# Linear attention whose state is kept compact, 64x64 a head, with a fused update out of PSUM

## The chip, the cores and the metric

The kernel runs on one core of one Trainium2 chip. What is measured is the device time of one execution, in microseconds. Engines are named as the profile names them: PE is TensorE's matmul, PEld its weight load, DVE is VectorE, ACT is ScalarE, POOL is GpSimd, SP is SyncE, which issues most of the DMAs.

## What is computed

Three layers stand one behind the other: a linear attention with a decaying state, a mixture of eight experts of which each token takes one, and a gated feed-forward layer. Only the first is touched:

```python
B, H, S, D = r.shape                      # 4, 8, 768, 48
state = np.zeros((B, H, D, D))
for t in range(S):
    kt, vt, rt = (k[:, :, t], v[:, :, t], r[:, :, t])
    cur = np.einsum('bhd,bhe->bhde', u[None] * kt, vt)
    y[:, :, t] = np.einsum('bhd,bhde->bhe', rt, state + cur)
    state = w[None, :, :, None] * state + np.einsum('bhd,bhe->bhde', kt, vt)
```

The 4 x 768 tokens of 384 = 8 x 48 numbers then go through the experts (384 to 1024 to 384) and through the last layer (384 to 1536 to 384), all in float32.

## The kernel before

**Tiles.** The attention works on tiles of 128 tokens: six tiles make one batch element, and four of those make 24 tiles. In a tile the eight heads lie as four pairs (`NP = 4`). A pair takes 128 partitions: head j of a pair has its 48 dimensions in partitions 64j to 64j + 47, and the 16 behind them are padding. Within a tile the recurrence over time is replaced by products. With `pw[t]` the decay to the power t, r is multiplied by the powers (`rdT`, on DVE) and k by their inverses (`kdT`, and token by token `kdc`, on POOL).

**The steps of one tile, by function.** `scores` forms k by r for each head (`pss`, L406): the two heads of a pair use 64 rows of the array each and write two PSUM banks. DVE then copies the masked scores into `dsb`, which already holds the diagonal term with u (L410). `state` forms the tile's sum of k by v in `pskv` (L428, one 48x48 product a head, the two heads of a pair side by side in the columns of the array) and brings the state forward: it adds `pskv` to the old state (L435) and multiplies the sum by the tile's whole decay `w128` (L441), once for each half j of the partitions. `outputs` multiplies the state by `rdT` (L453) and the values by `dsb` (L460) into one PSUM tile `psy`, which ACT copies to `yT` (L465). `rows_out` and `emit` (L114 to L127) form the gate's logits and store the rows.

**The state's form.** `st_b` is two buffers of 128x(4x128). Each pair has a 128x128 block that is zero but for two 48x48 squares on its diagonal, one a head, so that one 128x128 product serves both heads. POOL clears both buffers at the start (L332), and only the squares are ever written. The DVE instructions of `state` work on 48 partitions and 4x48 columns.

**What sets the order.** PE, DVE, ACT and POOL issue the attention in program order. One round of the loop over i runs: `scaled_r(i+1)`, `bonus(i+1)`, `scores(i)`, `state(i-1)`, `scaled_k(i+2)`, `outputs(i-1)`, `rows_out(i-2)`. What a product of the state in `outputs` reads was thus written a round earlier. Between these steps `advance()` issues, one at a time, small DVE instructions that sort the finished batch element's tokens to their experts (`route`, `gate`); `state` calls it after each of its DVE instructions, twice where `i >= HURRY` (18). The first tile of a batch element (c = 0) has no old state, and the last (c = 5) forms no new one. Both the experts and the last layer come behind the attention.

Of the kernel before, what the change touches and what calls it, by code (L numbers as in the profile page):

```python
# [9 lines left out]
F32 = mybir.dt.float32  # L10
# [5 lines left out]
ALU = mybir.AluOpType  # L16
# [4 lines left out]
P = 128  # L21
# [15 lines left out]
def moe_kernel(ctx, tc, cst, small, tok, tr, u, w1, w2, m_gate, m_val, m_out, out):  # L37
    nc = tc.nc
    NT, DM = out.shape
    H, D = u.shape  # L40
# [3 lines left out]
    NP = H // 2  # L44
# [19 lines left out]
    ident, mask, iota_p, niota, rev8, slot, tokid, tile_i, part_i, ltm = (  # L64
        cs[:, at[n]] for n in ("ident", "mask", "iota", "niota", "rev", "slot", "tokid", "tile", "part", "ltm")
    )
# [196 lines left out]
    with ExitStack() as actx:  # L263
# [53 lines left out]
        for q in range(NP):  # L317
            nc.vector.tensor_tensor_scan(
                out=pw[:, q, 1:], data0=wc[:, q : q + 1].to_broadcast([P, P]), data1=ones,
                initial=1.0, op0=ALU.mult, op1=ALU.mult,  # L320
            )
            nc.vector.reciprocal(wkT[:, q, :], pw[:, q, 1:])
        pst = ps_m.tile([P, NP, P], F32, name="pst", tag="m")
        for q in range(NP):
            nc.tensor.transpose(pst[:, q, :], wkT[:, q, :], ident)
        wk_tok = carve(H * D).rearrange("p (h d) -> p h d", d=D)
        nc.scalar.copy(wk_tok, pst.rearrange("p q (j d) -> p (q j) d", j=2)[:, :, 0:D])

        nc.gpsimd.memset(yd_all[:, used[0] :], 0.0)
        st_b = [acst.tile([P, NP, P], F32, name=f"st{i}") for i in range(2)]  # L330
        for t in st_b:
            nc.gpsimd.memset(t, 0.0)  # L332
        w128 = pw[:, :, P : P + 1].to_broadcast([P, NP, D])
        nc.vector.memset(rows_f, 0.0)
        nc.vector.memset(cum[:, 0:1, :], 0.0)

# [11 lines left out]
        def inputs(i):  # L348
            t = io[i % NIO]
            r_t, k_t = heads(t[:, 0 : RK // 2]), heads(t[:, RK // 2 : RK])  # L350
            rT, kT = pairs(t[:, RK : RK + T]), pairs(t[:, RK + T :])
            rdT = apool.tile([P, NP, P], F32, name="rdT", bufs=3)
            kdT = apool.tile([P, NP, P], F32, name="kdT", bufs=3)
            ck = apool.tile([P, H, D], F32, name="ck")
            kdc = apool.tile([P, H, D], F32, name="kdc", bufs=3)
            S[i] = r_t, k_t, rT, kT, rdT, kdT, ck, kdc

        def scaled_k(i):

            if i >= NTILE:  # L360
                return
            inputs(i)
            r_t, k_t, rT, kT, rdT, kdT, ck, kdc = S[i]
            if i == 0:
                for q in range(NP):
                    nc.gpsimd.tensor_tensor(out=kdT[:, q], in0=kT[:, q], in1=wkT[:, q], op=ALU.mult)
                    nc.gpsimd.tensor_tensor(out=rdT[:, q], in0=rT[:, q], in1=wrT[:, q], op=ALU.mult)
            eng = nc.vector if i < EARLY else nc.gpsimd
            eng.tensor_tensor(out=ck, in0=k_t, in1=u_tok, op=ALU.mult)
            eng.tensor_tensor(out=ck, in0=ck, in1=r_t, op=ALU.mult)  # L370
            if i:
                nc.gpsimd.tensor_tensor(out=kdT, in0=kT, in1=wkT, op=ALU.mult)
            nc.gpsimd.tensor_tensor(out=kdc, in0=k_t, in1=wk_tok, op=ALU.mult)

        def scaled_r(i):
            if i >= NTILE:
# [41 lines left out]
        def state(i):  # L418
            c = i % NCH
            if c + 1 == NCH:  # L420
                return
            rdT, kdT, kdc, dsb, v_t = S[i]
            st, st_n = st_b[i % 2], st_b[(i + 1) % 2]
            pskv = ps_m.tile([P, NP, 64], F32, name="pskv", tag="m")
            for q in range(NP):
                for j in range(2):
                    p0 = 64 * j
                    nc.tensor.matmul(  # L428
                        pskv[p0 : p0 + D, q, 0:D], lhsT=kdc[:, 2 * q + j, :], rhs=v_t[:, 2 * q + j, 0:D],
                        start=True, stop=True,  # L430
                    )
            js = [(slice(64 * j, 64 * j + D), slice(64 * j, 64 * j + D)) for j in range(2)]
            if c:
                for pr, cl in js:
                    nc.vector.tensor_tensor(out=st_n[pr, :, cl], in0=pskv[pr, :, 0:D], in1=st[pr, :, cl], op=ALU.add)  # L435
                    advance()
                    if i >= HURRY:
                        advance()
            for pr, cl in js:
                src = st_n[pr, :, cl] if c else pskv[pr, :, 0:D]  # L440
                nc.vector.tensor_tensor(out=st_n[pr, :, cl], in0=src, in1=w128[pr], op=ALU.mult)  # L441
                advance()
                if i >= HURRY:
                    advance()

        def outputs(i):
# [3 lines left out]
            psy = ps_y.tile([P, NP, P], F32, name="psy", tag="y")  # L450
            if c > 0:
                for q in range(NP):
                    nc.tensor.matmul(  # L453
                        psy[:, q, :], lhsT=st_b[i % 2][:, q, :], rhs=rdT[:, q, :], start=(q == 0), stop=False,
                        skip_group_check=True,
                    )
            for q in range(NP):
                for j in range(2):
                    p0 = 64 * j
# [912 lines left out]
```

## Time and profile before

| | |
|---|---|
| median of 3 runs | 865.82 us (865.14 to 867.04) |
| the profiled execution's own time | 865.42 us |
| its span, first to last instruction | 863.6 us |
| PE busy | 825.0 us, 96% of the span |
| DVE busy | 550.7 us, 64% |
| ACT busy | 348.7 us, 40% |
| POOL busy | 215.9 us, 25% |

The attention fills the first 160 us; the experts and the last layer fill the rest. A share of busy time is a mean over both. "Busy" counts an instruction from its start to its end, also where it is held up in between, and the records of PE overlap, since matmuls are pipelined. On PE one float32 product is two records.

### The profile page before, as it was taken

The numbers are of one execution on the slowest core, as the hardware profiler recorded it, in microseconds if no ns is written. First come the engines' busy times: TensorE is split into PE (matmuls) and PEld (weight loads), VectorE is DVE, ScalarE is ACT, GpSimd is POOL, SyncE is SP. The second block draws the span as 40 slices with busy tenths as digits, with TensorE's granted clock in tenths as the row PEclk, the third lists the DMA queues.
The fourth block names the chain that finished last, engine by engine and source line by source line (L and its number), as shares of the span: only waits on it lengthen the run. The fifth ranks groups of instructions, "written<-read, shape, count | busy, mean of one in ns | idle before, by whom it ended". The sixth has DMA issues, their size and how long they took to land.

```text
span 863.6 us, 14276 instructions
## 1 busy us (share of the span) xinstructions
PE 825.0 (96%) x5375; PEld 740.3 (86%) x5376; DVE 550.7 (64%) x1101; ACT 348.7 (40%) x789; POOL 215.9 (25%) x205
## 2 busy tenths in 40 slices
PE   7988877999999999999999999999999999999995
PEld 5766656899899999999888888888888888889995
DVE  8999999759999898974555333533533343344532
ACT  3665655446556646654343212211221221222321
POOL 7986764155334242110000200100010010001000
PEclk7998999999999999999999999999999999999998
DMA  8787766456688786642330100000010010001000
GB/s 302 258 304 230 261 229 206 132 170 195 194 277 241 250 256 212 199 123 68 110 95 27 38 1 1 31 18 1 13 37 2 1 33 10 1 8 38 1 20 22
DMA packets 61838, 99.55 MB, mean 115 GB/s; under 512 B 5364, under 2 KB 47872, under 8 KB 61760
## 3 DMA queue, kind: packets, MB, share of 16 engines
q1 hardware_dynamic: 58320, 88.44, 31.9%
q0 software_dynamic: 3440, 10.11, 3.6%
q8 instruction: 44, 0.72, 0.4%
q14 instruction: 34, 0.28, 0.1%
HBM read 82.00 MB, written 16.53 MB: 114 GB/s over the span
## 4 chain that ended last, share of the span: by engine, by line
issue 57%; DVE 18%; PE 13%; DMA 5%; POOL 3%; ACT 2%; SPq 0%; DVEq 0%; POOLq 0%; ACTq 0%
DMA m<-ab 3%; PE py L1068 3%; PE ph L1068 2%; POOL out_dram L1212 2%; DVE dsb L410 2%; DVE st L441 2%; DMA yd_all<-in_tr_dram 2%; DVE rdT L380 2%; DVE w1l L946 2%; DVE ab L922 1%; PE pya L1068 1%; PE psy L460 1%; PE psy L453 1%; DVE ab L918 1%; DVE h L1088 1%
## 5 line engine op out<-in xcount | busy, mean ns | idle before, releaser
L1236 DVE TENSOR_TENSOR hv<-pg,hv 128x512 f32<-128x512 f32 (+1 forms) x84 | 51.6, 615 | 156.8 <-ACT hv L1235 156.7
L1212 POOL DMA_INDIRECT out_dram<-ot,tokd x24 | 24.8, 1035 | 452.3 <-DVE ot L1211 448.7
L1235 ACT ACTIVATE hv<-pg 128x512 f32<-128x512 f32 (+1 forms) x84 | 45.1, 537 | 169.3 <-PE pg L1231 169.0
L854 ACT CAST hh<-hv 128x512 fp32r<-128x512 f32 (+1 forms) x84 | 47.0, 559 | 141.3 <-DVE hv L1237 141.3
L1205 PE MATMUL po<-wh,hh 128*128 128x384 f32 x288 | 97.1, 337 | 0.0
L1205 PE MATMUL po<-wh,hl 128*128 128x384 f32 x288 | 97.0, 337 | 0.0
L1205 PE MATMUL po<-wl,hh 128*128 128x384 f32 x288 | 97.0, 337 | 0.0
L1231 PE MATMUL pg<-xh,wh 128*128 128x512 f32 (+1 forms) x252 | 91.1, 362 | 0.0
L1068 PE MATMUL ph<-x,w1h 128*128 128x416 f32 x336 | 91.0, 350 | 0.0
L1231 PE MATMUL pg<-xh,wl 128*128 128x512 f32 (+1 forms) x252 | 90.9, 361 | 0.0
L1231 PE MATMUL pv<-xh,wh 128*128 128x512 f32 (+1 forms) x252 | 90.8, 360 | 0.0
L1231 PE MATMUL pv<-xh,wl 128*128 128x512 f32 (+1 forms) x252 | 90.7, 360 | 0.0
L1231 PE MATMUL pv<-xl,wh 128*128 128x512 f32 (+1 forms) x252 | 90.6, 360 | 0.0
L1231 PE MATMUL pg<-xl,wh 128*128 128x512 f32 (+1 forms) x252 | 90.5, 359 | 0.0
L1068 PE MATMUL py<-h,w2h 128*128 128x416 f32 x336 | 89.7, 352 | 0.0
L396 ACT ACTIVATE dsb<-cs,cb 128x128 f32<-128x128 f32 x192 | 58.8, 389 | 54.9 <-DVE cb L392 54.9
L855 DVE TENSOR_TENSOR hl<-hv,hh 128x512 fp32r<-128x512 f32 (+1 forms) x84 | 51.7, 616 | 45.4 <-ACT hh L854 45.1
L1237 DVE TENSOR_TENSOR hv<-pv,hv 128x512 f32<-128x512 f32 (+1 forms) x84 | 51.7, 615 | 43.4 <-PE pv L1231 42.7
L919 POOL TENSOR_TENSOR low<-low,exw 128x384 f32<-128x384 f32 x36 | 40.3, 1120 | 106.5 <-DVE exw L915 87.5
L1068 PEld LDWEIGHTS py<-h,w2h 128*128 128x128 f32 x336 | 62.9, 188 | 0.8
L1068 PEld LDWEIGHTS ph<-x,w1h 128*128 128x128 f32 x336 | 63.0, 188 | 0.5
L1068 PE MATMUL ph<-x,w1l 128*128 128x416 f32 x168 | 60.7, 361 | 2.6 <-DVE h L1088 2.6
(211 smaller groups left out, 1774.9 us busy)
## 6 DMA issues: line engine op xcount, KB each, us to landing
r<-in_w_dram SPq DMA_DIRECT2D x64, 384.0 KB
yd_all<-in_tr_dram SPq DMA_DIRECT2D x24, 512.0 KB
yd_all<-in_tok_dram SPq DMA_DIRECT2D x24, 384.0 KB
m<-ab SPq DMA_DIRECT2D x36, 192.0 KB
rw<-m SPq DMA_DIRECT2D x36, 192.0 KB
yd_all<-in_tok_dram SPq DMA_DIRECT2D x24, 256.0 KB
x_d<-xt SPq DMA_DIRECT2D x24, 192.0 KB
cva<-in_w_gate_dram SPq DMA_DIRECT2D x12, 384.0 KB
```

Of the source, the lines that this page charges most:

```text
L380: nc.vector.tensor_tensor(out=rdT, in0=rT, in1=wrT, op=ALU.mult)
L396: nc.scalar.mul(dsb[:, h, :], ident, cb[:, h : h + 1])
L854: first = nc.scalar.copy(hi, src)
L855: second = nc.vector.tensor_tensor(out=lo, in0=src, in1=hi.bitcast(F32), op=ALU.subtract)
L919: nc.gpsimd.tensor_tensor(out=low, in0=low, in1=ex.bitcast(F32), op=ALU.mult)
L1068: nc.tensor.matmul(dst[:, 0:n], lhsT=a, rhs=b, start=start and t == 0, stop=stop and t == 2)
L1205: nc.tensor.matmul(po[t], lhsT=a[:, t * P : (t + 1) * P], rhs=bb, start=(f == 0 and j == 0), stop=(f == KF2 - 1 and j == 2))
L1212: st = nc.gpsimd.indirect_dma_start(out=out[:, :], out_offset=bass.IndirectOffsetOnAxis(ap=tokd[:, i : i + 1].bitcast(U32), axis=0), in_=o ...
L1231: nc.tensor.matmul(dst, lhsT=a[:, fs], rhs=bb[:, q, :], start=(q == 0 and j == 0), stop=(q == KD - 1 and j == 2))
L1235: nc.scalar.activation(hv, pg, AF.Sigmoid)
L1236: nc.vector.tensor_tensor(out=hv, in0=pg, in1=hv, op=ALU.mult)
L1237: nc.vector.tensor_tensor(out=hv, in0=pv, in1=hv, op=ALU.mult)
```

## The change

The state is held as 128x(4x64): head j of pair q has its 64x64 square in partitions 64j to 64j + 63 and columns 64q to 64q + 63, and no zeros lie between. The decay of the whole tile is moved into the keys: `we` is the inverse powers times the power 128 (four ACT instructions in the set-up), and `wk_tok`, from which POOL makes `kdc`, is now the transpose of `we`. So `pskv` comes out already decayed, and one DVE `scalar_tensor_tensor` for a pair does old state times decay plus `pskv`: four instructions of 128x64 in place of four of 48x192. For c = 0 one copy of 128x256 takes the place of two multiplications. The products that form `pskv` are 64x64 instead of 48x48, for which `kdc` gets zero padding, written once into three standing buffers. The products that read the state are two of 64x64 for a pair, where one of 128x128 stood.

```diff
+        we = apool.tile([P, NP, P], F32, name="we", tag="yT")
+        for q in range(NP):
+            nc.scalar.mul(we[:, q, :], wkT[:, q, :], pw[:, q, P : P + 1])
         for q in range(NP):
-            nc.tensor.transpose(pst[:, q, :], wkT[:, q, :], ident)
+            nc.tensor.transpose(pst[:, q, :], we[:, q, :], ident)
...
-        st_b = [acst.tile([P, NP, P], F32, name=f"st{i}") for i in range(2)]
-        for t in st_b:
-            nc.gpsimd.memset(t, 0.0)
-        w128 = pw[:, :, P : P + 1].to_broadcast([P, NP, D])
+        st_b = [acst.tile([P, NP, 64], F32, name=f"st{i}") for i in range(2)]
+        kdc_b = [acst.tile([P, H, 64], F32, name=f"kdc{i}") for i in range(3)]
+        for t in kdc_b:
+            nc.gpsimd.memset(t[:, :, D:], 0.0)
...
-            nc.gpsimd.tensor_tensor(out=kdc, in0=k_t, in1=wk_tok, op=ALU.mult)
+            nc.gpsimd.tensor_tensor(out=kdc[:, :, 0:D], in0=k_t, in1=wk_tok, op=ALU.mult)
...
                     nc.tensor.matmul(
-                        pskv[p0 : p0 + D, q, 0:D], lhsT=kdc[:, 2 * q + j, :], rhs=v_t[:, 2 * q + j, 0:D],
+                        pskv[p0 : p0 + 64, q, :], lhsT=kdc[:, 2 * q + j, :], rhs=v_t[:, 2 * q + j, :],
                         start=True, stop=True,
                     )
-            js = [(slice(64 * j, 64 * j + D), slice(64 * j, 64 * j + D)) for j in range(2)]
-            if c:
-                for pr, cl in js:
-                    nc.vector.tensor_tensor(out=st_n[pr, :, cl], in0=pskv[pr, :, 0:D], in1=st[pr, :, cl], op=ALU.add)
-                    advance()
-                    if i >= HURRY:
-                        advance()
-            for pr, cl in js:
-                src = st_n[pr, :, cl] if c else pskv[pr, :, 0:D]
-                nc.vector.tensor_tensor(out=st_n[pr, :, cl], in0=src, in1=w128[pr], op=ALU.mult)
+            if c == 0:
+                nc.vector.tensor_copy(st_n, pskv)
+                advance()
+                advance()
+                return
+            for q in range(NP):
+                nc.vector.scalar_tensor_tensor(
+                    out=st_n[:, q, :], in0=st[:, q, :], scalar=pw[:, q, P : P + 1], in1=pskv[:, q, :],
+                    op0=ALU.mult, op1=ALU.add,
+                )
                 advance()
                 if i >= HURRY:
                     advance()
...
                 for q in range(NP):
-                    nc.tensor.matmul(
-                        psy[:, q, :], lhsT=st_b[i % 2][:, q, :], rhs=rdT[:, q, :], start=(q == 0), stop=False,
-                        skip_group_check=True,
-                    )
+                    for j in range(2):
+                        pr = slice(64 * j, 64 * j + 64)
+                        nc.tensor.matmul(
+                            psy[pr, q, :], lhsT=st_b[i % 2][pr, q, :], rhs=rdT[pr, q, :], start=(q == 0), stop=False,
+                            skip_group_check=True,
+                        )
```

Two places show what stands in a row. On DVE, in the fourth batch element, instructions of the sorting (`rk` to `sel`) lie between those of the state. Before:

```order
L127 TENSOR_REDUCE lg_1970<-psl_2019 128x16
L178 TENSOR_TENSOR rk<-psp,oh_all 128x48
L435 TENSOR_TENSOR st_160<-pskv,st_159 48x4x48
L181 TENSOR_REDUCE rank_all<-rk 128x6
L185 SCALAR_TENSOR_TENSOR num<-rank_all,at_e 128x6
L435 TENSOR_TENSOR st_160<-pskv,st_159 48x4x48
L189 TENSOR_SCALAR big<-num 128x6
L192 SCALAR_TENSOR_TENSOR npos<-big,num 128x6
L194 TENSOR_SCALAR col<-big 128x6
L441 TENSOR_TENSOR st_160<-st_160,yd_all 48x4x48
L199 TENSOR_TENSOR p_oh<-cs,npos 128x768
L202 TENSOR_TENSOR sel<-cs,col 128x192
```

The same place of the changed kernel:

```order
L127 TENSOR_REDUCE lg_2016<-psl_2065 128x16
L178 TENSOR_TENSOR rk<-psp,oh_all 128x48
L442 SCALAR_TENSOR_TENSOR st_165<-st_164,yd_all,pskv 128x64
L181 TENSOR_REDUCE rank_all<-rk 128x6
L185 SCALAR_TENSOR_TENSOR num<-rank_all,at_e 128x6
L442 SCALAR_TENSOR_TENSOR st_165<-st_164,yd_all,pskv 128x64
L189 TENSOR_SCALAR big<-num 128x6
L192 SCALAR_TENSOR_TENSOR npos<-big,num 128x6
L194 TENSOR_SCALAR col<-big 128x6
L442 SCALAR_TENSOR_TENSOR st_165<-st_164,yd_all,pskv 128x64
L199 TENSOR_TENSOR p_oh<-cs,npos 128x768
L202 TENSOR_TENSOR sel<-cs,col 128x192
```

The sorting's instructions keep their places; each of the four state instructions is exchanged for one of the new form.

On PE, one tile of the first batch element from its last product of the logits on. Before:

```order
L126 MATMUL psl_410<-cs,lT 128x128
L428 MATMUL pskv<-yd_all,kdc 48x48 x8
L453 MATMUL psy<-rdT,st_159 128x128 x4
L460 MATMUL psy<-dsb,yd_all 64x128 x8
L114 MATMUL psl<-yT,sm_t 32x128 x4
```

The same place of the changed kernel:

```order
L126 MATMUL psl_417<-cs,lT 128x128
L432 MATMUL pskv<-yd_all,kdc_168 64x64 x8
L459 MATMUL psy<-rdT,st_164 64x128 x8
L466 MATMUL psy<-dsb,yd_all 64x128 x8
L114 MATMUL psl<-yT,sm_t 32x128 x4
```

Nothing moves; four products of the state become eight, all into the tile `psy`.

## Rows read from the trace of the kernel before

**Rows 1.** Stretches, one per batch element: busy us (instructions) by engine, granted clock, DMA

```profile
23.20:53.80 30.60, 28.44 (x371) 22.50 (x370) 29.89 (x47) 21.16 (x68) 28.73 (x26) 0.96 0.74 254
53.80:89.90 36.10, 30.64 (x387) 24.43 (x386) 35.33 (x76) 19.44 (x59) 25.28 (x23) 0.91 0.78 260
89.90:130.50 40.60, 32.78 (x403) 26.22 (x403) 39.76 (x88) 24.14 (x72) 27.42 (x24) 0.92 0.71 244
130.50:160.00 29.50, 25.41 (x328) 20.73 (x329) 27.04 (x79) 16.48 (x52) 12.19 (x10) 0.94 0.53 177
```

The columns behind the stretch and its length are PE, PEld, DVE, ACT, POOL, then the granted clock as a share of full speed, the DMA engines' busy share and GB/s.

**Rows 2.** The same stretches, DVE instructions that touch the state alone: busy us (count)

```profile
23.20:53.80 30.60, 10.55 (x18) 0.96 0.74 254
53.80:89.90 36.10, 8.42 (x16) 0.91 0.78 260
89.90:130.50 40.60, 8.51 (x18) 0.92 0.71 244
130.50:160.00 29.50, 6.34 (x18) 0.94 0.53 177
```

**Rows 3.** The tile st: its DVE instructions, ns least/median/most

```profile
L435 DVE TENSOR_TENSOR st<-pskv,st x32: 324/351/361, 24.5 to 156.3; 48x192 f32<-48x192 f32 x32
L441 DVE TENSOR_TENSOR st<-st,yd_all x32: 340/382/1318, 25.2 to 157.1; 48x192 f32<-48x192 f32 x32
```

**Rows 4.** DVE's timeline in the first batch element: start us, length us, instruction

```profile
30.34 0.20 DVE L127 TENSOR_REDUCE lg<-psl 128x16 f32<-128x64 f32 x1
30.47 0.72 DVE L435 TENSOR_TENSOR st<-pskv,st 48x192 f32<-48x192 f32 x2
31.22 1.72 DVE L441 TENSOR_TENSOR st<-st,yd_all 48x192 f32<-48x192 f32 x2
32.97 1.38 DVE L380 TENSOR_TENSOR rdT<-yd_all 128x512 f32<-128x512 f32 x1
```

**Rows 5.** PE's timeline, one tile without a wait, at full clock

```profile
26.10 0.66 PE L120 MATMUL psx<-cs,yT 128*128 128x128 f32 x4
26.69 1.16 PE L406 MATMUL pss<-rdT,kdT 64*128 64x128 f32 x16
...
28.04 0.56 PE L428 MATMUL pskv<-yd_all,kdc 128*48 128x48 f32 x16
28.53 1.16 PE L453 MATMUL psy<-rdT,st 128*128 128x128 f32 x8
29.62 1.09 PE L460 MATMUL psy<-dsb,yd_all 128*64 128x128 f32 x16
...
31.00 0.66 PE L120 MATMUL psx<-cs,yT 128*128 128x128 f32 x4
```

**Rows 6.** PE's timeline behind a wait for the sorting, at the lower clock

```profile
74.44 0.48 PE L210 MATMUL psw<-sel,p_oh 128*128 128x64 bf16 x6 [2.89 <-DVE sel L206]
...
75.93 2.08 PE L453 MATMUL psy<-rdT,st 128*128 128x128 f32 x8
```

**Rows 7.** Groups by shape: DVE instructions with a PSUM input; busy us, mean ns

```profile
L1088 DVE SCALAR_TENSOR_TENSOR h<-ph,h 128x416 fp32r<-128x416 f32 x56 | 32.6, 581 | 5.1 <-ACT h L1087 4.9 <-issue 0.2
...
L1211 DVE COPY ot<-po 128x384 f32<-128x384 f32 x12 | 6.7, 557 | 12.9 <-DMA out_dram<-ot,tokd 10.7 <-PE po L1205 1.9
...
L1088 DVE SCALAR_TENSOR_TENSOR h<-pha,h 128x256 fp32r<-128x256 f32 x8 | 3.4, 423 | 3.1 <-ACT h L1087 2.6 <-issue 0.3
...
L212 DVE SCALAR_TENSOR_TENSOR rows_f<-psw,rows_f 128x32 f32<-128x32 f32 x4 | 0.7, 173 | 0.0
```

**Rows 8.** Timeline of the set-up: the token decay and the first kdc

```profile
8.78 0.48 ACT L327 COPY yd_all<-pst 128x384 f32<-128x384 f32 x1 [6.72 <-PE pst L325]
...
12.18 2.60 POOL L373 TENSOR_TENSOR kdc<-yd_all 128x384 f32<-128x384 f32 x2
```

**Rows 9.** Stretches behind the attention, columns as in the first group

```profile
160.00:200.00 40.00, 39.35 (x321) 37.35 (x318) 27.17 (x86) 21.66 (x56) 14.55 (x15) 1.00 0.55 166
200.00:350.00 150.00, 145.94 (x797) 138.99 (x797) 140.52 (x289) 88.54 (x174) 57.21 (x51) 1.00 0.76 236
```

More of the change, by code (lines that the diff above doesn't have):

```diff
@@ L354, in inputs @@
             ck = apool.tile([P, H, D], F32, name="ck")
-            kdc = apool.tile([P, H, D], F32, name="kdc", bufs=3)
+            kdc = kdc_b[i % 3]
             S[i] = r_t, k_t, rT, kT, rdT, kdT, ck, kdc
```

## The prediction

> **What bounds the kernel now.** I began with the stretches of the attention, one per batch element [rows 1]. In the first three DVE is busy 29.89 of 30.60 us, 35.33 of 36.10 and 39.76 of 40.60: 98% each time. PE is busy 28.44, 30.64 and 32.78 us of the same, POOL 28.73, 25.28 and 27.42. In the fourth DVE has 27.04 of 29.50 and PE 25.41. So the attention is set by DVE, with PE not far below. Behind it the rule is another: PE is busy 39.35 of 40 us and 145.94 of 150 [rows 9]. Those stages start when the attention hands over and run at PE's pace, so what the attention gains or loses should reach the end of the span almost whole.
>
> Then I took out DVE's part for the state [rows 2]: 10.55, 8.42, 8.51 and 6.34 us, together 33.8 of the 136.8 us. The reader is to see in [rows 3] that its two kinds of instruction behave differently at the same shape, 48x192. The addition, one input in PSUM and one in SBUF, takes 324 to 361 ns in all 32 cases. The multiplication, both inputs in SBUF, takes 340 to 1318 ns. In a plain tile of the first batch element two additions take 0.72 us and two multiplications 1.72 us [rows 4], while POOL is nearly always busy [rows 1]. `rdT`, which also reads two tensors of SBUF, follows there with 1.38 us. I read the excess as DVE being held while POOL works on SBUF.
>
> Last comes PE's floor, from a tile that it does without a wait at full clock [rows 5]: from one `psx` (26.10) to the next (31.00) is 4.90 us. The reader is to compare three products in it. The scores have 16 records of 64 rows and take 1.16 us. The values by `dsb`, 16 records of 64 columns, take 1.09. The state's product has only 8 records of the full array, and takes 1.16. So two products on different halves of the array's rows, or of its columns, run side by side and cost one.
>
> **The change part by part.** *DVE, the state.* Four instructions of 128x64 replace four of 48x192, in 16 tiles of 24. No row shows this form: one SBUF tensor, one PSUM tensor and a scalar for each partition. The nearest are `scalar_tensor_tensor` out of PSUM with a constant scalar [rows 7]: 173 ns at 32 columns, 423 at 256, 581 at 416. The last two give (581 - 423) / 160 = 0.99 ns a column, so 64 columns take 173 + 32 x 0.99 = 205 ns alone. In [rows 4] the addition starts at 30.47, 0.07 us before the `lg` in front of it ends at 30.54. Overlapped like this, one would follow the other after 0.13 us, and four cost 3 x 0.13 + 0.21 = 0.60 us. Back to back without overlap, as the two additions stand (0.72 us for two of 0.35), they cost 0.82. I take 0.60, since the two additions begin on different partitions and the new four on the same, as `lg` and the addition do. The ends for the range are 0.5 and 0.9. For c = 0 a copy out of PSUM takes 557 ns at 384 columns, so 557 - 128 x 0.99 = 0.43 us at 256, against about 0.7 for two of 0.35. A batch element then spends 4 x 0.60 + 0.43 = 2.8 us on the state instead of 10.55, 8.42, 8.51 and 6.34.
>
> *The state's products on PE.* Two 64x64 products for each pair use opposite halves of rows and columns at once, and both write the tile `psy`. No row shows that combination: pairs by rows write two banks (`pss`), and pairs by columns share all rows (`psy` from `dsb`). Both run side by side at the price of one, so I take 1.16 us as before. Below it there is little to find, since the columns that stream through are the same. The upper bounds are in the second rival. `pskv` streams 64 columns instead of 48: its 16 records in eight pairs take 0.56 us, at most a third more is 0.2, and I take 0.1. PE's floor for a tile is then 5.0 us, less 0.5 where c = 5 forms no `pskv`, and 5.0 - 1.1 = 3.9 where c = 0 has no state to read. Some 0.8 us for the sorting's products in all but the first batch element makes 4 x 5.0 + 4.5 + 3.9 = 28.4 or 29.2 us a batch element.
>
> The page "TensorEngine Tiling (Array Packing)" of the Trainium skill speaks against this part: its section on restrictions says that different row tiles can't use one PSUM bank at the same time. By that the two products of a pair would not run side by side, which is the second rival. The page "PSUM — Partial Sum Buffer" of the Trainium skill, in its section on bank collisions, calls the bank of each partition a RAM of its own and reports no clash between different groups of partitions in one bank, which is the case here; by that the price stays as I took it. No run here shows either yet.
>
> *POOL.* `kdc` has as many elements as before and only lands with gaps. I count zero, and 0.1 us more a tile as the upper end, which POOL's idle time in the later three stretches covers (10.8, 13.2 and 17.3 us [rows 1]). The three paddings replace two clearings before the first tile's inputs are there.
>
> *The set-up.* `wk_tok` now waits for four ACT scalings and is one step later. Before, its copy ends at 8.78 + 0.48 = 9.26, and `kdc` uses it first at 12.18 [rows 8]. The 2.9 us between cover the extra step, which at ACT's pace in the same row is about half a us. I count zero; without that cover it would cost 0.5 us.
>
> *The sum.* For each stretch I set DVE's busy time with the new state against PE's floor and take the later, plus what the two can't overlap. First stretch: DVE 29.89 - 10.55 + 2.8 = 22.1, PE 28.4, so PE decides: 30.6 becomes 28.4, a gain of 2.2. Second: DVE 35.33 - 8.42 + 2.8 = 29.7, PE 29.2. Two engines so even don't overlap wholly; I put 31, a gain of 5. Third: DVE 39.76 - 8.51 + 2.8 = 34.1, PE 29.2; I put 35, a gain of 5.6. Fourth: PE stands still for 29.50 - 25.41 = 4.1 us, and I take 2.5 of it. Together 15.3 us.
>
> From this I take back a part. A multiplication that no longer waits for POOL brings the next one with two SBUF inputs, mostly `rdT`, to POOL's instruction sooner, so some of the wait only moves. Read from [rows 2] and [rows 3], the state cost 8.42 us in the second stretch, where 16 instructions of 0.35 would be 5.6, and 8.51 in the third, where 18 would be 6.3: 5 us of waits in the two. I give back 3. So 12 us are gained: the profiled execution of 865.42 becomes 853.4, and since the median of the runs lies 0.4 above it, I predict **854 us**.
>
> The clock can add to the gain. In the second stretch PE waits 2.89 us for the sorting's `sel` and then runs the state's product in 2.08 us instead of 1.16, at the lower of the two clock levels (1.2 instead of 2.4 GHz) [rows 6, 5]. The granted clock of the four stretches is 0.96, 0.91, 0.92 and 0.94 [rows 1]. If shorter waits bring back half of what is missing, that is about 0.03 x 136.8 = 4 us. I leave it out of the sum and take it as the lower end.
>
> **The rivals.** *First: the freed time on DVE is taken by others.* DVE's waits for POOL then move whole, and POOL, with 28.73 busy of 30.60 us in the first stretch, holds its pace. For it speaks `rdT`, which is held in the tile shown. Against it, the additions were never held, and the new form has the same two kinds of input. The page "SBUF — State Buffer" of the Trainium skill, section on who interferes with whom, says that with at most one SBUF input there is no contention, but leaves open for me whether a scalar out of SBUF counts; by the rows it need not. Price: the gains of the second and third stretch shrink by the 5 us of waits, and with four instructions at 0.9 us by another 16 x 0.3 = 5. That leaves 15.3 - 10 = 5, and 2 if the first stretch gives nothing: 861 to 864 us.
>
> *Second: the two products of a pair take turns.* Place: PE, in `outputs`, 20 tiles. Taking turns, 16 records cost twice 1.16, so 1.1 us more a tile. PE's floor is then 28.4 + 5 x 1.1 = 33.9 in the first stretch, 3.3 above today's 30.6; the second comes to about 35 (a gain of 1), the third to 36.5 (4), and the fourth loses 2. All in all it comes to about zero: 866 us. From there on the kernel is **slower than before**. If each turn also costs what a change of the array's division does, the step grows further. The upper bound for that is the row at the lower clock: 2.08 for 8 records, thus 4.2 for 16, 3.0 more a tile. The stretches would be 28.4 + 15 = 43, 44, 44 and 25.4 + 15 = 40 us, 34 us slower, 900 us. The point at which it decides is 1.1 us a tile; I see 868 to 880 as its likelier part. Against it: pairs by rows and pairs by columns each run side by side [rows 5].
>
> *Third: the change gains more,* because the clock holds: 846 to 848 us, as worked out above.
>
> **How the numbers follow.** I give the forecast (849 to 860) 0.62, the third rival (below 849) 0.10, the first (860 to 864.1) 0.13, and taking turns 0.11: 0.05 for about the time before, 0.06 for slower. The rest, 0.04, is for causes that I don't see, half of them slower, half without an effect. A measurement of this kernel can tell a difference of about 0.2%, which is 1.7 us. Faster by more is 0.62 + 0.10 + 0.13 = 0.85, of which I move 0.03 to no change, since the first rival ends at the bound. So faster 0.82, same 0.05 + 0.02 + 0.03 = 0.10, slower 0.06 + 0.02 = 0.08. The range from 846 to 864 leaves out the second rival and a little below, less than 0.2.
>
> **What would show it.** In the changed profile the state's DVE instructions should sum to about 11 us, each near 0.2 us and none above 0.3; if many reach 1 us, the scalar counts as an SBUF input. The state's 16 records should take 1.1 to 1.2 us in a tile without a wait; 2.2 or more means that they take turns. A tile without a wait should take about 5.0 us on PE, the first scores of the experts should start some 12 us earlier, and the stages behind should last as long as before. The prediction is wrong if PE's waits for `sel` and for `dsb` stay as long as they are, or if the stages behind the attention give back what it gained.

## The result and the profile after

The changed kernel takes 855.67 us (median of 4 runs, 854.55 to 856.34), the kernel before 866.43 in the same series (865.14 to 867.65): a ratio of 0.9875, with an interval from 0.9856 to 0.9894. That is 10.8 us less, where 12 were forecast. The profiled execution took 855.75 us, with a span of 854.0, where before had 865.42 and 863.6. So the two traces differ by 9.6 us, and the stages below account for these. Over the whole span PE is busy for 820.0 us, DVE for 534.2, ACT for 350.9 and POOL for 215.7.

The same four stretches of the attention as in [rows 1], with the same columns, cut at the same work (the last one ends, as there, where PE starts on `psx` of the last tile but one):

```profile
22.60:50.40 27.80, 26.42 (x402) 20.73 (x398) 21.83 (x48) 23.59 (x74) 27.33 (x25) 1.00 0.88 298
50.40:82.30 31.90, 28.84 (x427) 22.99 (x426) 31.76 (x77) 18.91 (x57) 27.99 (x25) 0.95 0.84 290
82.30:120.20 37.90, 32.88 (x443) 26.22 (x443) 37.76 (x86) 24.19 (x72) 27.65 (x24) 0.91 0.77 261
120.20:148.48 28.28, 25.52 (x369) 20.27 (x369) 24.66 (x78) 16.48 (x52) 11.25 (x10) 0.94 0.56 185
```

They are 2.8, 4.2, 2.7 and 1.2 us shorter, 10.9 in all, and the first begins 0.6 us earlier. In the first, DVE now has room (21.83 of 27.80), while PE (26.42, at a granted clock of 1.00 where it was 0.96) and POOL (27.33) are both nearly full. Some of PE's records are missing there (402). A second profile of the same kernel, from the last run below, has 420 of them in the same stretch, and in it PE never stands still. POOL's busy time contains waits of its own: `kdc` takes 986 to 1712 ns at one shape.

```profile
22.36:50.10 27.74, 27.74 (x420) 22.00 (x416) 21.82 (x47) 23.51 (x74) 27.27 (x25) 0.98 0.89 297
```

In the second and third DVE is as full as before: 31.76 of 31.90 and 37.76 of 37.90. The state alone on DVE, as in [rows 2]:

```profile
22.60:50.40 27.80, 3.80 (x17) 1.00 0.88 298
50.40:82.30 31.90, 3.91 (x16) 0.95 0.84 290
82.30:120.20 37.90, 4.30 (x17) 0.91 0.77 261
120.20:148.48 28.28, 4.48 (x17) 0.94 0.56 185
```

That is 16.5 us where 33.8 stood. The tile `st`, as in [rows 3] (ns least, median, most):

```profile
L459 PE MATMUL psy<-rdT,st x320: 269/269/473, 21.6 to 146.9; 64*64 64x128 f32 x160
L442 DVE SCALAR_TENSOR_TENSOR st<-st,yd_all,pskv x64: 241/269/286, 24.4 to 144.2; 128x64 f32<-128x64 f32 x64
L437 DVE COPY st<-pskv x4: 403/406/446, 21.2 to 121.6; 128x256 f32<-128x256 f32 x4
```

All 64 fused updates lie between 241 and 286 ns, where the multiplications reached 1318: none is held, although beside 46 of them an instruction of POOL runs. DVE's timeline in a plain tile, to be read beside [rows 4]:

```profile
33.60 0.21 DVE L127 TENSOR_REDUCE lg<-psl 128x16 f32<-128x64 f32 x1
33.73 0.84 DVE L442 SCALAR_TENSOR_TENSOR st<-st,yd_all,pskv 128x64 f32<-128x64 f32 x4
34.49 1.76 DVE L384 TENSOR_TENSOR rdT<-yd_all 128x512 f32<-128x512 f32 x1
```

Four updates take 0.84 us where additions and multiplications took 2.5. With the last at 0.27, the other three follow at steps of (0.84 - 0.27) / 3 = 0.19. `rdT` behind them now takes 1.76 us instead of 1.38. PE's timeline, one tile without a wait, as in [rows 5]:

```profile
30.50 0.66 PE L120 MATMUL psx<-cs,yT 128*128 128x128 f32 x4
31.09 1.16 PE L410 MATMUL pss<-rdT,kdT 64*128 64x128 f32 x16
...
32.44 0.69 PE L432 MATMUL pskv<-yd_all,kdc 128*64 128x64 f32 x16
33.05 1.09 PE L459 MATMUL psy<-rdT,st 64*64 64x128 f32 x16
34.07 1.09 PE L466 MATMUL psy<-dsb,yd_all 128*64 128x128 f32 x16
...
35.45 0.66 PE L120 MATMUL psx<-cs,yT 128*128 128x128 f32 x4
```

From `psx` to `psx` it is 4.95 us. The state's 16 records of 64x64 take 1.09, so the two products of a pair run side by side, on opposite quarters of the array and in one bank. `pskv` takes 0.69 instead of 0.56.

The experts' first product, of the kernel before and then of the changed one (ns least, median, most, first and last start):

```profile
L1068 PE MATMUL pha<-x,w1l x24: 277/280/387, 161.6 to 176.0; 128*128 128x256 f32 x24
```

```profile
L1074 PE MATMUL pha<-x,w1l x24: 277/280/384, 150.1 to 164.5; 128*128 128x256 f32 x24
```

It starts 11.5 us earlier. A product of the last layer, in the same order, has its first 12.2 and its last 12.1 us earlier:

```profile
L1231 PE MATMUL pg<-xh,wl x252: 277/389/397, 402.9 to 849.2; 128*128 128x512 f32 x90, 128*128 128x256 f32 x36
```

```profile
L1237 PE MATMUL pg<-xh,wl x252: 277/389/397, 390.7 to 837.1; 128*128 128x512 f32 x90, 128*128 128x256 f32 x36
```

The span is only 9.6 us shorter, so 2.5 us are lost behind PE's last product. They lie in POOL's sequence at the very end, where a branch passes over the code for tokens that found no place. POOL's part of that line, before and then after:

```profile
L846 POOLq EVENT_SEMAPHORE  x4: 17/17/43, 856.2 to 856.4; - x4
...
L846 POOLq COMPARE_BRANCH  x1: 45/45/45, 855.7 to 855.7; - x1
```

```profile
L852 POOLq EVENT_SEMAPHORE  x4: 17/17/43, 846.6 to 846.8; - x4
...
L852 POOLq COMPARE_BRANCH  x1: 53/53/53, 843.6 to 843.6; - x1
```

From the branch to POOL's next instruction of that line it is 0.5 us before and 3.0 after. What follows, up to the end of the span, is as long in both (863.6 - 856.2 = 7.4 and 854.0 - 846.6 = 7.4).

### The profile page after: what moved, and what is told of

Same layout as the page of the kernel before. It is cut to its first block, busy times and chain, and to the rows that moved or that the text cites. A ratio compares the mean times of both kernels' runs of the same rounds, so it can differ in the third digit from the quotient of the medians.

```text
span 854.0 us, 14581 instructions
## 1 busy us (share of the span) xinstructions
PE 820.0 (96%) x5535; PEld 736.6 (86%) x5536; DVE 534.2 (63%) x1097; ACT 350.9 (41%) x793; POOL 215.7 (25%) x206
## 4 chain that ended last, share of the span: by engine, by line
issue 58%; DVE 16%; POOL 10%; PE 8%; DMA 5%; ACT 1%; SPq 0%; POOLq 0%; DVEq 0%; ACTq 0%
DMA m<-ab 3%; POOL out_dram L1218 2%; POOL kdT L376 2%; DVE w1l L952 2%; POOL kdc L377 2%; DMA yd_all<-in_tr_dram 1%; DVE ab L928 1%; DVE ab L924 1%; DVE dsb L414 1%; POOL ck L373 1%; DVE w2l L952 1%; DVE ab L919 1%; DVE rdT L384 1%; PE pya L1074 1%; DVE h L1094 1%
```

## The experiments

The theory after the result: the gain comes from DVE's update alone, the form of the products neither costs nor gives anything, and the rest of the freed DVE time is taken up because POOL and PE now limit together with DVE. The rival: the products, too, have a part in it, or DVE alone still sets the time. The medians below stand beside the kernel before in the same series, which took 868.94 us in the first group of runs (products alone, update alone, two steps, half the turns), 867.19 in the second (no update, update twice, decay on ACT, sorting later) and 865.52 in the last (the other four). The kernel before alone moves by 3.4 us from series to series, so medians of two series are compared by their ratios to it. Edits are against the changed kernel, but for the first.

**The products alone.** The kernel before, with the compact state and the 64x64 products, and the old additions and multiplications:

```diff
-        st_b = [acst.tile([P, NP, P], F32, name=f"st{i}") for i in range(2)]
+        st_b = [acst.tile([P, NP, 64], F32, name=f"st{i}") for i in range(2)]
...
-                    nc.tensor.matmul(
-                        psy[:, q, :], lhsT=st_b[i % 2][:, q, :], rhs=rdT[:, q, :], start=(q == 0), stop=False,
...
+                    for j in range(2):
+                        pr = slice(64 * j, 64 * j + 64)
+                        nc.tensor.matmul(
+                            psy[pr, q, :], lhsT=st_b[i % 2][pr, q, :], rhs=rdT[pr, q, :], start=(q == 0), stop=False,
```

> The kernel before with the compact state and the two 64x64 products a pair alone; DVE's update stays as it was: two additions and two multiplications of 48x192. My theory, that the gain is DVE's: DVE's 33.8 us for the state stay, PE's product of the state is 0.07 us shorter a tile (1.09 against 1.16), 1.4 us at most where PE sets the pace, so 864.5 to 866.5 us, 0 to 1.5 below before. The rival, that the smaller products on PE bring the gain: near the changed kernel, 855 to 859 us.

871.55 us against 868.94, a ratio of 1.0018 (1.0001 to 1.0035). The products bring nothing by themselves, not even the small gain that I expected: the experts start 1.4 us later (163.0 for 161.6).

**The update alone.** The changed kernel, but with one 128x128 product for each pair:

```diff
-                    for j in range(2):
-                        pr = slice(64 * j, 64 * j + 64)
-                        nc.tensor.matmul(
-                            psy[pr, q, :], lhsT=st_b[i % 2][pr, q, :], rhs=rdT[pr, q, :], start=(q == 0), stop=False,
...
+                    flat = st_b[i % 2].rearrange("p q d -> p (q d)")
+                    nc.tensor.matmul(
+                        psy[:, q, :], lhsT=flat[:, 64 * min(q, 2) : 64 * min(q, 2) + 128], rhs=rdT[:, q, :],
+                        start=(q == 0), stop=False, skip_group_check=True,
```

> The changed kernel, but the state is read by one 128x128 product a pair, as before; the product reads the squares of two neighbouring pairs, so the attention's values are other ones, while every instruction's shape and every wait is that of the mixed kernel. My theory: nearly the whole gain stays, 855.5 to 857.5 us, the 64x64 products being worth at most 1.4 us. The rival, that the products bring it: 862 us or more.

857.75 us, a ratio of 0.9875 (0.9851 to 0.9899), the same as for the whole change. The experts start at 150.4 us, as in the changed kernel (150.1). So the whole gain is the update's. The products only serve it: they read a state that has no zeros.

**The update in two steps.** Is it the fused form that matters, or the compact shape?

```diff
-            for q in range(NP):
-                nc.vector.scalar_tensor_tensor(
...
+                    nc.vector.tensor_tensor(
+                        out=st_n, in0=st, in1=pw[:, :, P : P + 1].to_broadcast([P, NP, 64]), op=ALU.mult
+                    )
...
+                    nc.vector.tensor_tensor(out=st_n, in0=pskv, in1=st_n, op=ALU.add)
```

> The changed kernel, but the fused update is taken apart: one multiplication of 128x256 with both inputs in SBUF, then one addition of 128x256 with one input in PSUM. Alone they need about 0.35 + 0.4 us a tile, no more than the 0.84 us of the four fused ones, so a theory by DVE's own work alone says no change, 854.5 to 856.5 us. My theory says that the multiplication is held while POOL reads SBUF, up to some 1.3 us each, and some of that reaches the time: 857 to 860 us.

860.29 us, a ratio of 0.9893 (0.987 to 0.9916). Its instructions on the tile `st`:

```profile
L443 DVE TENSOR_TENSOR st<-st,yd_all x16: 413/894/1478, 24.2 to 146.7; 128x256 f32<-128x256 f32 x16
L447 DVE TENSOR_TENSOR st<-pskv,st x16: 409/419/425, 25.3 to 147.2; 128x256 f32<-128x256 f32 x16
```

At one shape, on one engine, in one kernel, the step with two inputs in SBUF takes 413 to 1478 ns and the one with an input in PSUM 409 to 425. That is what I had read out of [rows 3]. What holds it is POOL: of the 16 multiplications, the four that have no instruction of POOL beside them take 413 to 422 ns, the twelve that have one 469 to 1478. Here is one of the twelve with POOL's instruction, which ends 0.29 us before it, and then one of the four:

```profile
33.93 1.04 DVE L443 TENSOR_TENSOR st<-st,yd_all 128x256 f32<-128x256 f32 x1
33.68 1.00 POOL L374 TENSOR_TENSOR ck<-ck,yd_all 128x384 f32<-128x384 f32 x1
...
135.35 0.42 DVE L443 TENSOR_TENSOR st<-st,yd_all 128x256 f32<-128x256 f32 x1
```

The Trainium skill says the same ("SBUF — State Buffer", Who interferes with whom): a DVE instruction with two SBUF inputs contends with POOL's reads, one with at most one does not, as long as it is outside the modes that take both of DVE's ports. The trace agrees, and it answers for this kernel what I had left open there: the scalar out of SBUF doesn't count, as the 64 updates of 241 to 286 ns show. In time the held step costs little: the experts start at 152.7 us instead of 150.1. So most of the gain also comes with two DVE instructions on the compact state in place of four, and some 2.6 us of it with the fused form.

**Half the turns.** The products of all upper halves, then of all lower ones:

```diff
-                for q in range(NP):
-                    for j in range(2):
-                        pr = slice(64 * j, 64 * j + 64)
+                for j in range(2):
+                    pr = slice(64 * j, 64 * j + 64)
+                    for q in range(NP):
```

> The changed kernel with the state's eight products of a tile in another order: the four of the upper halves first, then the four of the lower, so that neighbours use the same part of the array and must take turns. It prices the rival of the prediction: the 16 records should take about 2.1 us instead of 1.09 in a tile without a wait. By the prediction's sum (PE's floor 1.0 us higher in 20 tiles, gain about zero) 864 to 867 us. If PE had slack in the stretches in which DVE is busy throughout, only the first and the last stretch grow: 859 to 863 us.

The 16 records take 1.58 us instead of 1.09, not twice as long, as I had thought: some of the lower ones still run beside upper ones.

```profile
33.71 1.58 PE L459 MATMUL psy<-rdT,st 64*64 64x128 f32 x16
```

862.31 us, a ratio of 0.9917 (0.9896 to 0.9939); the experts start 3.9 us later than in the changed kernel. 20 x 0.49 = 9.8 us more on PE cost 3.9, and I took 0.4 for the price of each.

**Full turns.** The second rival whole: the eight products of the values by `dsb` stand between the two halves.

```diff
+            from_state(0)
             for q in range(NP):
...
+            from_state(1)
```

> The changed kernel with the state's products apart by halves: first the four of the upper halves, then the eight products of the values by dsb, then the four of the lower halves, so that no two products of the state from opposite halves of rows and columns can stand beside each other. Nothing is left out. This is the whole price of my second rival, about 1 us of PE in each of 20 tiles. By the sum of the prediction (PE the bound of the first stretch and near it in the others), 864 to 867 us. By the slope that the run with half the turns showed, about 0.4 us of time for each us on PE, 20 us cost 7 to 8: 862 to 863. If PE has room behind DVE and POOL, 856 to 858.

```profile
28.62 1.08 PE L458 MATMUL psy<-rdT,st 64*64 64x128 f32 x8
29.64 1.09 PE L467 MATMUL psy<-dsb,yd_all 128*64 128x128 f32 x16
30.66 1.08 PE L458 MATMUL psy<-rdT,st 64*64 64x128 f32 x8
```

870.92 us, a ratio of 1.0063 (1.0033 to 1.0094): slower than before. A tile takes 1.02 us more, 20 tiles 20.4, and the experts start 15.8 us later (165.9). Its stretches:

```profile
22.49:54.93 32.44, 32.44 (x420) 25.81 (x416) 20.95 (x47) 23.69 (x74) 29.54 (x27) 1.00 0.74 246
54.93:87.95 33.02, 31.94 (x427) 25.73 (x426) 32.26 (x77) 19.08 (x57) 25.67 (x23) 1.00 0.86 291
87.95:132.20 44.25, 40.88 (x402) 32.50 (x399) 36.32 (x87) 25.75 (x75) 27.16 (x23) 0.77 0.67 223
```

PE is busy for all of the first, which becomes 4.6 us longer for five tiles. In the third the granted clock falls to 0.77, and a part of its 6.3 us is that. All three expectations were too low. The slope of the run before misled me most; the sum in the prediction gave about the time before (866), 5 us too little, and its remark that 868 to 880 is likelier had this case right.

**No update.** Only one column is copied in place of the updates; both buffers of the state are cleared at the start, and the copies for c = 0 stay. The wrong values send the kernel into its path for left-over tokens behind the last layer (1018.0 us in all), so only its attention can be compared.

```diff
+            nc.vector.tensor_copy(st_n[:, 0, 0:1], pskv[:, 0, 0:1])
             for q in range(NP):
-                nc.vector.scalar_tensor_tensor(
...
```

> The changed kernel without the 64 fused updates (only a copy of one column of pskv is left in a tile, and the products read a state that isn't brought forward), so the attention's values are other ones. DVE has 64 x 0.19 = 12 us less. If DVE still sets the pace in the two middle stretches (busy 31.8 of 31.9 and 37.8 of 37.9 us), 3 to 4 us less in each and some 1 in the last: 847 to 851 us. If PE or POOL took over there, as the rival has it: 854 us or more.

Without the updates the experts start only 1.8 us earlier (148.2), as I expected it if POOL or PE took over. The first, third and fourth stretch are 1.1, 1.0 and 1.0 us shorter, and the second is 0.9 longer. The second stretch, and in it `rdT` and the sorting's `key` on DVE:

```profile
49.64:82.43 32.79, 27.92 (x427) 21.83 (x426) 32.42 (x65) 19.53 (x59) 28.92 (x26) 1.00 0.81 284
```

```profile
49.64:82.43 32.79, 6.14 (x5) 1.00 0.81 284
```

```profile
49.64:82.43 32.79, 3.17 (x4) 1.00 0.81 284
```

DVE has lost 3.9 us of work and is busier than ever, 32.42 of 32.79. In the changed kernel the five `rdT` took 4.88 there and the four `key` 2.02; here they take 6.14 and 3.17. Beside each of the three long `rdT` (1.48 to 1.79 us, where the other two take 0.68) an instruction of POOL runs for most of its time. The wait for POOL has moved on to such instructions.

**The update twice.** Each fused update is issued two times, with the same result.

```diff
+                for _ in range(2):
+                    nc.vector.scalar_tensor_tensor(
```

> The changed kernel with each fused update issued twice, to the same result: 12 us more for DVE, 0.77 a tile, all of it out of PSUM and so without waits for POOL. My theory: the first stretch, where DVE is busy 21.8 of 27.8 us, takes it for nothing, the two middle ones grow by 3 each, the last by 1: 861 to 864 us. If DVE set the pace throughout: 867. If it no longer set it anywhere: 856.

867.3 us, a ratio of 0.9998 (0.9982 to 1.0014): the whole gain is gone. My theory's 861 to 864 was too low; the time is that of the rival in which DVE sets the pace throughout (867), but the first stretch, as the theory has it, takes the work for nothing. In a plain tile the eight take 2.10 us instead of 0.84. The stretches show where it costs:

```profile
22.41:50.21 27.80, 27.55 (x420) 21.71 (x416) 24.28 (x63) 23.40 (x74) 27.33 (x25) 0.99 0.87 298
50.21:85.61 35.40, 30.00 (x427) 23.57 (x426) 34.70 (x92) 18.55 (x57) 27.18 (x25) 0.95 0.75 261
85.61:126.36 40.75, 33.60 (x443) 25.76 (x443) 40.05 (x102) 23.91 (x72) 26.99 (x24) 0.92 0.74 243
126.36:158.99 32.63, 26.03 (x369) 20.66 (x369) 29.35 (x94) 16.48 (x52) 11.58 (x10) 0.95 0.48 161
```

Nothing in the first, where DVE has room beside PE and POOL; 3.5, 2.9 and 4.4 us in the second, third and fourth. The experts start 10.5 us later for 12.4 us more of DVE's busy time. The theory had 3 us right for the two in the middle and took 1 for the fourth, where DVE is not full and the cost is still almost all of the 4.7 us added; why is open. Together with the run before: DVE's time costs almost its full length when it is added, and gives almost nothing when more of it is removed. The changed kernel stands at the knee.

**POOL's `kdc` twice.** Is POOL the other limit?

```diff
             nc.gpsimd.tensor_tensor(out=kdc[:, :, 0:D], in0=k_t, in1=wk_tok, op=ALU.mult)
+            nc.gpsimd.tensor_tensor(out=kdc[:, :, 0:D], in0=k_t, in1=wk_tok, op=ALU.mult)
```

> The changed kernel with POOL's multiplication for kdc issued twice into the same place (nothing is left out). It adds some 1.0 to 1.2 us to POOL in each of 24 tiles, about 27 us in all, and to no other engine. Theory: with DVE relieved, POOL, busy 27 to 28 us of each of the first three stretches, holds up DVE's instructions with two SBUF inputs and limits the attention together with DVE and PE, which is why removing more DVE work gained almost nothing: several us slower than the changed kernel, 860 to 866. Rival: POOL has slack and only DVE and PE count: 855 to 857, as the changed kernel itself.

868.92 us, a ratio of 1.0041 (1.0024 to 1.0058). Some 24 us on an engine that is busy a quarter of the span cost 13.6 us against the changed kernel in the same series, and the experts start 16.3 us later.

```profile
24.22:58.64 34.42, 29.41 (x410) 22.75 (x409) 20.70 (x48) 20.69 (x66) 33.48 (x31) 0.97 0.81 247
58.64:94.30 35.66, 29.79 (x402) 23.31 (x399) 34.74 (x77) 19.32 (x59) 34.72 (x31) 0.89 0.78 254
```

The first stretch is 6.6 us longer for six instructions of 1.0 us, and POOL is busy 33.48 of it. So there POOL is a limit together with PE. In the second POOL and DVE are both full. The third is 3.9 us longer, and the fourth, where POOL is busy for less than half, 0.5. That is the theory's answer, somewhat stronger than expected.

**The decay on ACT.** Old state times decay on ACT, the addition on DVE:

```diff
-                nc.vector.scalar_tensor_tensor(
...
+                nc.scalar.mul(st_n[:, q, :], st[:, q, :], pw[:, q, P : P + 1])
+            nc.vector.tensor_tensor(out=st_n, in0=pskv, in1=st_n, op=ALU.add)
```

> The changed kernel, but ACT multiplies the state by the decay (four instructions of 128x64 a tile) and DVE adds pskv in one instruction of 128x256. DVE's part falls from 0.84 to about 0.45 us a tile, 6 us in all; ACT's grows by about 1 us a tile and stays below PE's. If DVE sets the pace in the middle stretches, 3 us less: 852 to 854 us. If DVE's addition now waits for ACT, which issues in order: 855 to 858 us.

866.77 us, a ratio of 0.9998 (0.9986 to 1.001): the gain is gone, against both expectations. The instructions are short (334 ns on ACT, 424 on DVE), but ACT issues in order, and the four stand behind its long work for `dsb`. DVE's longest wait in the attention (us in total, times, longest):

```profile
DVE st L443 <- ACT st L442: 24.2, 12, 3.0
```

PE's longest, 9.3 us in ten, is for ACT as well.

A less busy engine was no help, since the wait in its queue is longer than what it took off DVE.

**The sorting's products later.** PE's waits for `sel` remain: 5.7 us in three, 6.4 before. They are issued a step later, first while the first two batch elements are sorted (the condition ends in round 18 of the loop; the second expectation below speaks of three), then for the first alone:

```diff
-                if kind != tensor or kind and since > now[0] - 2:
+                if kind != tensor or kind and since > now[0] - (3 if now[0] < 3 * 19 else 2):
```

```diff
-                if kind != tensor or kind and since > now[0] - 2:
+                if kind != tensor or kind and since > now[0] - (3 if now[0] < 3 * 13 else 2):
```

> The changed kernel, but in the first 18 rounds PE may take the sorting's products only three counts of the loop after DVE has been told to prepare them, not two: in two of three batch elements they stand behind the logits' products, half a round later. If PE's waits for sel (5.7 us in three, and the lower clock behind them) hold up the attention, 851 to 854 us; if DVE alone sets the pace there, no change, 855 to 856.5 us.

> The changed kernel, with the products that wait for the sorting (psw) issued a step later while the first batch element is sorted, that is in the second stretch alone. With this rule in force for three batch elements the second stretch became 2.8 us shorter, and the third and fourth 1.8 and 4.0 longer. If the second stretch's gain stands by itself: 852 to 854 us. If the later stretches give it back because the work left over piles up there: 855 to 857.

> The changed kernel itself, on the same chip as the three others, so that differences of a few us can be read against it. Expected: 855 to 857 us, ratio to the kernel before 0.986 to 0.989, a start of the experts near 150 us, and a last layer about 2 us longer than before, with the clock falling to its lower level some 10 us before the end.

The first takes 857.07 us, 0.9881 (0.9856 to 0.9906); the second 854.39, 0.987 (0.9838 to 0.9902); the changed kernel beside it 855.32, 0.9871 (0.9846 to 0.9896). In the first the waits for `sel` are gone and the second stretch is 2.8 us shorter, but PE then waits for `dsb` (6.9 us in eight), and the third and fourth are 1.8 and 4.0 longer. (Its trace is of the slowest of its four executions, 859.87 us, so these may be more than is usual.) In the second run, of the three waits one of 2.2 us is left, and the stretches are 27.79, 30.19 and 38.67 us: 1.7 us won in the second, 0.8 lost in the third. Neither can be told from the changed kernel. So the waits for `sel` were not what set the time.

## Why the prediction was right, and where its steps were off

The main step held: the attention's time is DVE's, and the new update takes it off. The products gain nothing by themselves (first two runs). That the time came out within 2 us is in part luck, since errors of several terms cancel. Point by point:

**The fused update** was mis-sized. I took steps of 0.13 us and 0.60 for four; they have 0.19 and 0.84, near the upper end of 0.9, and where instructions of the sorting stand between them each takes its full 0.27. The copy was right (0.41 for 0.43). So a batch element spends 3.8 to 4.5 us on the state instead of 2.8, and the four stretches 16.5 instead of 11.2.

**What was given back** was right in size. Taking the state out, DVE's other work grew in the second stretch from 35.33 - 8.42 = 26.91 to 31.76 - 3.91 = 27.85 us, and in the third from 31.25 to 33.46: 3.2 us, for 3 in the sum. It moves to instructions with two SBUF inputs, and not to these alone. The sorting's `sel` in the second stretch goes from the first of these rows to the second, and `rdT` in the third from the third to the fourth:

```profile
53.80:89.90 36.10, 1.53 (x3) 0.91 0.78 260
```

```profile
50.40:82.30 31.90, 2.89 (x3) 0.95 0.84 290
```

```profile
89.90:130.50 40.60, 5.98 (x6) 0.92 0.71 244
```

```profile
82.30:120.20 37.90, 6.79 (x6) 0.91 0.77 261
```

Of the 1.36 us that `sel` gained, 0.74 fell on a `tensor_scalar` (L206), which reads one tensor of SBUF: 1.00 us where it took 0.25. The sorting's `big`, a `tensor_scalar` with one tensor of SBUF and two constants, takes 164 to 172 ns three times and 931 once, in the third stretch, with POOL's `ck` beside it until shortly before its end:

```profile
L189 DVE TENSOR_SCALAR big<-num x4: 164/172/931, 61.7 to 153.9; 128x6 f32<-128x6 f32 x4
```

`eo` (L231), another of this kind, takes 1.06 us in two of its four cases, with `kdT` beside it, and 0.18 to 0.19 in the others. So one input in SBUF does not by itself keep an instruction from being held; that the updates never were holds for their form. The first rival is true in part. Without the updates it is true almost wholly. (The 2 us in its price should read 3: 15.3 - 10 - 2.2.)

**The second and third stretch** came out 4.2 and 2.7 us shorter, where 5 and 5.6 less the 3 were forecast, 7.6 in all. The sum, 6.9, is near; two errors cancel. The updates cost 2.6 us more there than I took. On the other side I had allowed 31 - 29.7 and 35 - 34.1, 2.2 us, for DVE and PE not overlapping, and DVE stands still for only 0.14 us in each.

**The first stretch** gained 2.8 for 2.2, and the floor of a tile is 4.95 us for 5.0. PE does decide there, busy for all of 27.74 us in the second profile. But that was only half of it: POOL, which I held for "nearly always busy" and yet counted at nothing, decides with it, as the doubled `kdc` shows. **The fourth** gained 1.2 us, half of the 2.5 that I took of PE's idle time; from its end to the experts' first product it is 1.57 us in both kernels.

**The state's products** cost 1.09 us for the 1.16 taken, `pskv` 0.13 more for 0.1. The rule on row tiles and banks that I had weighed ("TensorEngine Tiling (Array Packing)", Gotcha 1: PSUM Pressure, in the Trainium skill) does not hold for these products: both halves write one bank and run side by side. What I had set against it was a weaker support than I made of it: the section on bank collisions of "PSUM — Partial Sum Buffer" in the Trainium skill reports the missing clash for two engines, and repeats the rule on row tiles for TensorE's own writes. The price of the second rival was right all the same: where the two really take turns, it is 1.02 us a tile for the 1.1 taken, and the kernel is slower than before, by 5.4 us or 0.6%, where the sum came to about zero.

**The clock** gave little: 1.00, 0.95, 0.91 and 0.94 for 0.96, 0.91, 0.92 and 0.94. The waits for `sel` stayed (5.7 us for 6.4, and 2.8 for 3.9 for `dsb`), and behind them the state's product still runs at 1.2 GHz:

```profile
67.88 0.34 PE L210 MATMUL psw<-sel,p_oh 128*128 128x64 bf16 x6 [2.58 <-DVE sel L206]
...
68.91 1.97 PE L459 MATMUL psy<-rdT,st 64*64 64x128 f32 x16
```

The sign of being wrong that I had named, these waits staying as long as they are, nearly came although the forecast held. It was badly chosen: with the waits for `sel` gone or cut, the last runs above are no faster.

**The set-up and POOL** cost nothing, as counted: the first `kdc` starts at 12.64 us (12.18 before), the first stretch 0.6 us earlier.

**The stages behind** kept PE's pace, but not the end. The experts' and the last layer's products have won 12.1 us when the last of them starts, where 12 were forecast, and the tail, which no term of the sum had, takes 2.5 of it.

## What to carry to other kernels

An engine that is busy 98% of a stretch may be busy with waiting: look at the spread of its instructions' times at one shape, and put one input of those that are held into PSUM, or fold them into an instruction that has one tensor in PSUM and one in SBUF. Count what the others will then wait for, and test the knee from both sides: here doubling the update cost the whole gain, and removing it gained almost nothing, because the wait for POOL moved to other instructions and two other engines were nearly as full. A low share over the span (POOL's 25%) says nothing of the stretch that matters.

## What was not expected of the hardware

Two products on opposite quarters of the array and in one bank run side by side (1.09 us for 16 records), and in part also when the order goes by halves: with the four products of the upper halves ahead of the four of the lower ones, 16 records took 1.58 us, half of the turns that I had expected. Work between them makes the turns whole (2.16 us).

A `tensor_scalar` with one tensor in SBUF can be held beside POOL like an instruction with two (`big`: 931 ns for 164 to 172), while the fused update with one tensor in SBUF, one in PSUM and a scalar in SBUF never was.

The tail: POOL's branch over code that isn't run took 0.5 us before and 3.0 after. With the `kdc` issued twice, which adds 24 instructions to POOL's code and changes nothing else there, it is 0.5 again, and the 2.5 us are not lost:

```profile
L853 POOLq EVENT_SEMAPHORE  x4: 17/17/43, 859.2 to 859.4; - x4
...
L853 POOLq COMPARE_BRANCH  x1: 45/45/45, 858.7 to 858.7; - x1
```

In the nine other profiles with as many POOL instructions as the changed kernel has it is 3.0 to 3.1, in that of the products alone 1.8, and ACT's and DVE's branches over the same code take 2.8 to 3.6 us before and after: the 0.5 is the exception. So it goes with POOL's code and not with the work. That the place of the branch in the code decides whether the instructions behind it are already loaded is my reading; it was not tried by itself and stays open.
